# Scores of two tail heads in one run, bf16 maxima over partitions, a split last output, and a new order for five engines

## The chip, the cores and the metric

The kernel runs on one core of one Trainium2 chip. The metric is the device time of one execution in microseconds (us); every kernel is run several times and the median counts. Five engines work side by side, each through its own list of instructions in order: TensorE (PE; its weight loads are shown as PEld), VectorE (DVE), ScalarE (ACT), GpSimd (POOL) and SyncE (SP), which here only issues DMA transfers. A trace of one execution gives the start and the duration of each instruction.

## The reference, cut to what matters

```python
scores = scale * np.matmul(q, k.transpose(0, 1, 3, 2))     # B=4, H=8, S=576, D=64
a = softmax(np.where(causal, -1e9, scores))
local = np.matmul(a, v)
q_p = phi(q)                                                # elu(q) + 1
mem_out = (q_p @ M_prev) / (q_p . z_prev + 1e-6)
x = g * mem_out + (1 - g) * local                           # g = sigmoid(beta), per head
x = x.transpose(0, 2, 1, 3).reshape(2304, 512)
xn = x / sqrt(mean(x * x) + 1e-6) * rms_g
out = (silu(xn @ w_gate) * (xn @ w_val)) @ w_out            # 512 x 1536, 512 x 1536, 1536 x 512
```

## The kernel before, in words

The 2304 rows are cut into 18 blocks of 128. Each of the four sequences has 576 rows: four full blocks and 64 rows that are left. Two sequences share a **tail block**, so there are two of these, and in a tail block the upper 64 rows need the keys of one sequence and the lower 64 those of another. All matmuls of such a block therefore write 64 of the 128 output partitions, in pairs (`HALVES`); the text calls them half-column matmuls, since they use half of the array's columns.

A float32 product is made of three float16 products: each operand is split into a high and a low half (hi, lo), and hi·hi, hi·lo and lo·hi are added up in PSUM. Only the first four blocks run their attention in float32 (lines with `32` in their function's name). Before a split, a tensor is scaled by a power of two that a bound on its norms gives. For the bound, `gram` multiplies each tensor with itself on PE in bf16 (tile `csum`), DVE takes each partition's maximum (`mx`, `wmx`), and `over_partitions` spreads the maxima over all partitions: a matmul with the stationary operand `src[:, j]` repeated and an identity as the moving one (tile `allp`, L272).

A block and a group of heads are a unit of attention: `u_scores` (PE L626 for full blocks, L649 and L660 in `tail_scores`), a DVE instruction that scales, masks and reduces, `u_exp` on ACT (L689), `u_lo` (DVE L708, then one DMA transpose of the probabilities, tile `PT`), and `u_pv` (L739 to L741, and L757 for tail blocks). Memory reads are L794 (float32) and L855. Two blocks form a chunk of the MLP, nine chunks in all: `m_proj` (tile `gv`: 24 matmuls of 256 columns, float32 L1074 or float16 L1081), `m_act` (ACT L1098, DVE L1099 and L1102, which read the `gv` tile), `m_split` (hi and lo of the hidden layer, ACT L1119 and POOL L1120), `m_down` (tile `out`, L1147 or L1155 to L1157) and `put`, which scales the output into `res` and sends it.

PSUM has eight banks: the tags `sc`, `gv` and `out` have two each, and a tag's next tile waits until its bank's last reader is done. In a tail block each head takes one `sc` bank for the scores against the four full blocks of keys (16 matmuls) and then the other `sc` bank for those against the block's own rows (tile `sct`, 4 matmuls).

The order of each engine is written out by hand. `keep(kind)` puts a letter on the instructions that a function issues (S scores, P the product with V, M memory, G projection, D down projection and output DMA, Z `over_partitions`, l, m, b, d, W, B loads). The table `ISSUE` holds a string of such letters for each engine, and `issue_in_order` chains the instructions in that order: `S20` takes the next twenty of kind S, and `~n` skips n that are waiting.

Of the kernel before, what the change touches and what calls it, by code (L numbers as in the profile page):

```python
# [70 lines left out]
        "G3DGG2~1GD~1GDG4DGD3G5G2~3G4SG12S~7G5D~1GDG3D~1GD~2DG9S~7GS~7M~8SG3G~10MS~6GS2~6G5G~4GM2~7GG~2M~7S5S~1SM~7SDMM~6"
        "MM~5MGM2GMG2MG5S7G2SG4S2D~1GSGSG2S3MG3SGDG4DG12SG4SG3G2~1G9S6G8PZG5P2SGP4GPSP4S3P3SPSP2GP3GPGPG3SG14G2~3PGG~2S2G"
        "G3~1S2G~1G10S3S~1PM2S~1MGS~1S4MP3G2MPSGSPGP2MG~3MPGG~2GG2~1P2G~1PG5P4GP4GP2GPG4PGMGDG5DD2~1D2SDGD2~2MD~2D2MDG11D"
        "~2MGP2MPSGS~4SS~3P3G2MDPGSGDP3GS~2PS2MGSDGG~4DPG~4GMP5DPSPD~2G~3PG2P3GDMS~1GDGS3~1DS2DSG6PGDG3S2G3D~2GSG2SP8SGP3"
        "DPD2P10DS~1PS~1G~2D~3S~1G3~2PG~2GG~1GS~1DS~1SD2G3DGDGMD~3DG2D~2M2D~2GS~1GSGDG2M2G~6GSMDMSGDMG~4SG2SG~2G2SG2DG2D~"
        "1GMD~1SG3M2D~1MGD~4GDG3MDMGP5DP5GP7G2PGMD~1MPSP5SGDP3S~3DSGS~2GS~2DSDS2~1D~1P7DPSPSD2D~3DSG18D~2G3D~2G3S~5DG2SS~"
        "4GS2G2S2~2G3DPG3PGP2SPDP2GS~1PG3SPG5D2~2DPD~1DP5G~3PG~3S3G~3G3PG4S~4S3G4SG6DG3D~2PD~2G2DG~2GG4~1M2G2~1MG~1MD~1G~"
        "1P5MDGSPGMG2M2GPG2P2D~3P4GPS~4G3SP3SPG2SD~3SG2D2G~1GSG3MG2D~1DGSGSPDGP2S~2P2MP3GPG2PG~12GS2GPD~2PG4S2P2GSG2D~2SG"
        "~3G2PG6DMGMD~1MGM2P3SG2PSGDG2D~3G6P4MGPSPDPS3GSG2D3G2PSGDG3SGSGSGSG3SG4P3GDPDP2GPD~1PDGDG2P~1G~3P2G~3SG2SPSG~1PS"
        "~5G~1SGS~4P2SPS2PGSG5D~1G4PG5SG3D~1S2DGG2~1S4G2~1SG~1GD~1PGDGSPG2PDPD~1P2SPD~1P2SDGP4D~1GPSMS2GMP2GMD~1G4PG3D~1G"  # L80
# [33 lines left out]
    "Activation": (
        "K~2K~2K2fI~1T~1TITfT~1TE6ITE~2E~1E2E~1E~1EE~1E2U~3U~2U~19NU~1TU~12U~11NftTtU~15UTfET~1E~2E2U~8E~2E~1ETEUU~3TU~3E"
        "E~1E3UU~1UU~1U2E~1E2U~4U~1UoAU~12U2U~1oNU~1U~6U~4AUU~3U~2U2AU~4U~2U~1U2U~4U~4AUU~2U~1UXU~1UfUAUNU2AU2U~1UXc2U~1U"
        "cU2U~2AU~2cU~1UqAc2U~1UcU~1UxUcxUqxcxAcxU~1Ux2rxkxAU~1xkUxAcxkxFxcxAfxrxqAxHv3xAkE~1ECExFEACxO2HD~1HvAxvE2CAE2Dx"
        "CH~1E2AxHrCEyEkAyE~1CyH~1EfACNEyEHCv~1XFyqAEHyCEvCHAyEvrEyCHyNCAvfXysksyEHACqEFCAyEHrEC2HEO~1AEOCDHCAEHDANCXkEsH"
        "fECsAqCAFrHECE2CAHCEAHEC2HAECHNfAXksECsHAqFEHCEACrHEACECOHECAEOCHAENCsfHADXEskCHEACEAHCFEDCEHACsHseAqE~1EC2HvEAC"
        "HANXErAfCEHkAHCECkAHsAoECO~1FHEODCHAsE~1ECEAEvHvHCvDEAEs2HCAqE~1ECrHkfAHNAXFHs2AqfHArNECXECHE~1AkECHECEAFEHCsACs"  # L120
        "Es2CeEAHO~1qCOCAv~2DoHv~1Ev~1CE~1vAEvHDCHNCqAXECfErAHCEHACkAHkECHAFrHAkE~2HE~1ECEfNCEAqXE~2FE~1EHCACEHrAECHCAOE~"
        "1OD~2ECNHACfXkqHAE~1ECD~1HCAFErDHCEACHEAHCECAHECANfHXkAHAEFCECHAECEHACHO~1AECHOD~1E2CACHDAECHEACAHNECXECHAECHEAC"
        "HAHANXHAHAHAHOAHOAHAHDA2H2A2H2A2HADH2AHOD~2D~1D"
    ),
    "DVE": (
        ".~1f2.ZI~4JZIfI~3fS2.S2II~2I.~1IS2IS4TS2I2Su.2iSe~6SuSiTui2e~35u2iTiuie~26uiTi~1uiu~1iuiRU~1R2fJfZtZU~9S4UfS4Tfi"
# [1385 lines left out]
```

## Time and profile before

| | us |
|---|---|
| median of 3 runs | 594.09 (590.65, 594.09, 594.92) |
| the profiled execution | 592.08 |
| its span, first to last instruction | 590.4 |
| PE busy in the span | 577.9 |
| DVE, ACT, POOL busy | 427.4, 398.1, 129.3 |

The span is what the trace covers; the execution's own time is 1.7 us more. An engine is busy from an instruction's start to its end; matmuls overlap, so that PE's pitch (start to start) says more than the mean length of one. Views in use: busy time by stretch, waits by engine and line, the timeline, groups of instructions, and DMA issues.

### The profile page before, as it was taken

Reading aid. Unit: us, or ns where it says so; the run is one execution under the profiler, and the core shown is the slowest. Engines: PE = TensorE matmul, PEld = TensorE weight load, DVE = VectorE, ACT = ScalarE, POOL = GpSimd, SP = SyncE. Lnnn points to the kernel's source line nnn. Section 1 sums busy time; section 2 is a strip of 40 time slices with the busy share of each in tenths; the row PEclk is TensorE's granted clock in tenths of the full one; section 3 lists DMA queues with packets and bytes.
Section 4 is the critical chain, followed back from the end, with each engine's and each line's share of the span. In section 5 each row is a group of like instructions: output and inputs, shape, how many; then the busy total and the mean of one; then the engine's idle time right before and its main releaser. Section 6 shows DMA issues by size and latency. Waiting matters only on the chain.

```text
span 590.4 us, 15790 instructions
## 1 busy us (share of the span) xinstructions
PE 577.9 (98%) x6108; PEld 453.2 (77%) x6108; DVE 427.4 (72%) x1278; ACT 398.1 (67%) x856; POOL 129.3 (22%) x219
## 2 busy tenths in 40 slices
PE   8899999999999999999999999999999999999996
PEld 7898877678768778887777777777777777777773
DVE  5898779999998868776877676978866665742221
ACT  6899988878896757667667777866675555533211
POOL 2511100032332212121313231223122212121211
PEclk9999999999999999999999999999999999999999
DMA  8999794488598776887689678579685654340001
GB/s 264 326 374 382 251 225 114 83 189 206 116 166 162 145 138 133 151 157 144 104 156 180 140 127 166 118 134 156 117 172 84 91 110 100 69 87 19 18 1 54
DMA packets 183787, 87.57 MB, mean 148 GB/s; under 512 B 165792, under 2 KB 165792, under 8 KB 183712
## 3 DMA queue, kind: packets, MB, share of 16 engines
q1 hardware_dynamic: 180640, 81.82, 64.5%
q10 hardware_dynamic: 3072, 4.74, 2.5%
q8 instruction: 48, 0.79, 0.6%
q14 instruction: 27, 0.22, 0.1%
HBM read 37.77 MB, written 4.72 MB: 72 GB/s over the span
## 4 chain that ended last, share of the span: by engine, by line
PE 84%; DMA 9%; DVE 3%; ACT 2%; issue 1%; SPq 0%; ACTq 0%; DVEq 0%
PE gv L1081 38%; PE gv L1074 7%; PE out L1157 6%; PE out L1155 6%; PE out L1156 6%; PE sc L626 5%; DMA PT<-P 4%; PE out L1147 4%; DMA kv<-in_qkv_dram 2%; PE csum L299 2%; PE sc L649 1%; DMA M<-in_M_prev_dram 1%; PE loc L757 1%; PE loc L739 1%; PE loc L740 1%; PE loc L741 1%
## 5 line engine op out<-in xcount | busy, mean ns | idle before, releaser
L1081 PE MATMUL gv<-xT,wgv 128*128 128x256 f16 x2304 | 355.5, 273 | 0.6 <-DMA xT<-x 0.6
L1081 PEld LDWEIGHTS <-wgv 128*128 128x128 f16 x2304 | 209.5, 98 | 53.4 <-issue 3.5
L1120 POOL TENSOR_TENSOR h<-th,h 128x256 f16<-128x256 f32 x88 | 64.4, 734 | 258.4 <-ACT h L1119 224.7
L1098 ACT ACTIVATE th<-gv,wt 128x256 f32<-128x256 f32 x96 | 45.0, 469 | 71.6 <-PE gv L1081 68.2
L626 PE MATMUL sc<-kT,qT 128*128 128x128 f16 x576 | 91.7, 219 | 0.6 <-DMA qT<-qT 0.6
L1099 DVE SCALAR_TENSOR_TENSOR th<-th,gv 128x256 f32<-128x256 f32 x96 | 40.0, 417 | 71.0 <-ACT th L1098 69.3
L689 ACT ACTIVATE S<-S,nm 128x256 f32<-128x256 f32 (+3 forms) x112 | 70.3, 638 | 17.6 <-DVE nm L632 11.2
L708 DVE SCALAR_TENSOR_TENSOR P<-S,P 128x512 f16<-128x512 f32 (+2 forms) x96 | 65.6, 685 | 21.4 <-ACT P L203 21.3
L632 DVE CUSTOM_DVE_ANT_0 S<-sc,mask,qsc 128x256 f32<-128x256 f32 (+2 forms) x96 | 58.0, 613 | 15.3 <-PE sc L626 14.3
L1157 PE MATMUL out<-wo,h 128*128 128x512 f16 x176 | 65.8, 379 | 0.0
L1155 PE MATMUL out<-wo,h 128*128 128x512 f16 x176 | 65.6, 379 | 0.0
L203 ACT ACTIVATE P<-S 128x512 f16<-128x512 f32 (+2 forms) x96 | 58.1, 607 | 10.9 <-DMA PT<-P 7.4
L1156 PE MATMUL out<-wo,h 128*128 128x512 f16 x176 | 65.1, 379 | 0.0
L1119 ACT CAST h<-th 128x256 f16<-128x256 f32 x88 | 35.1, 399 | 42.3 <-DVE th L1102 28.0
L626 PEld LDWEIGHTS <-qT 128*128 128x128 f16 x576 | 51.9, 98 | 11.9 <-DMA qT<-qT 1.1
L739 PE MATMUL loc<-v,PT 128*128 128x65 f16 x288 | 50.6, 193 | 1.5 <-DMA PT<-P 1.4
L741 PE MATMUL loc<-v,PT 128*128 128x65 f16 x288 | 51.4, 193 | 0.0
L740 PE MATMUL loc<-v,PT 128*128 128x64 f16 x288 | 50.3, 193 | 0.0
L1074 PE MATMUL gv<-xT,wgv 128*128 128x256 f32 x192 | 47.3, 385 | 0.0
L1102 DVE SCALAR_TENSOR_TENSOR th<-th,wt,gv 128x256 f32<-128x256 f32 x96 | 45.7, 476 | 1.6
L1074 PEld LDWEIGHTS gv<-xT,wgv 128*128 128x128 f32 x192 | 34.7, 190 | 8.9 <-issue 4.5
L739 PEld LDWEIGHTS <-PT 128*128 128x128 f16 x288 | 28.0, 98 | 8.2 <-DMA PT<-P 2.8
(230 smaller groups left out, 988.4 us busy)
## 6 DMA issues: line engine op xcount, KB each, us to landing
kv<-in_qkv_dram SPq DMA_DIRECT2D x40, 256.0 KB, 3.9
q<-in_qkv_dram SPq DMA_DIRECT2D x18, 256.0 KB, 3.4
wo<-in_moe_w_out_dram SPq DMA_DIRECT2D x8, 512.0 KB, 5.1
out_dram<-res ACTq DMA_DIRECT2D x16, 256.0 KB, 2.9
wo<-in_moe_w_gate_dram SPq DMA_DIRECT2D x7, 512.0 KB, 6.8
wgv<-in_moe_w_val_dram SPq DMA_DIRECT2D x7, 512.0 KB, 7.3
qT<-qT SPq DMA_DIRECT2D x28, 128.0 KB, 2.8
wgv<-in_moe_w_gate_dram SPq DMA_DIRECT2D x5, 512.0 KB, 6.9
```

Of the source, the lines that this page charges most:

```text
L203: got = fn(*p, **k)
L626: nc.tensor.matmul(t[:, g * w + j * P : g * w + (j + 1) * P], qT[n][:, t2, h, :], kT[blk_of[(b, j)]][:, h, :], start=(t2 == 0), stop=(t2 = ...
L632: nc.vector.tensor_tensor_reduce(out=s[:, g * w : (g + 1) * w], in0=t[:, g * w : (g + 1) * w], in1=mask[:, m0 : m0 + w], scale=qsc[n][:, 5 ...
L689: nc.scalar.activation(v_, v_, AF.Exp, bias=nm[:, g : g + 1], scale=-1.0)
L708: m = nc.vector.scalar_tensor_tensor(out=p16[:, w : 2 * w], in0=s[:, :w], scalar=PSCALE, in1=p16[:, :w], op0=ALU.mult, op1=ALU.subtract)
L739: nc.tensor.matmul(a, phi_, vhi, start=(j == 0), stop=False)
L1074: nc.tensor.matmul(o, wgv[:, 1 + p, o0 : o0 + P], xT[0][:, cc, at], start=(cc == 0), stop=(cc == NC - 1))
L1081: nc.tensor.matmul(o, lhs, xT[c][:, rhs, :], start=(cnt == 0), stop=(cnt == 3 * NC - 1))
L1120: nc.gpsimd.tensor_tensor(h16[:, 1], th, h16[:, 0], ALU.subtract)
L1155: nc.tensor.matmul(o, hh, whi, start=(f == 0), stop=False)
L1156: nc.tensor.matmul(o, hh, wlo, start=False, stop=False)
L1157: nc.tensor.matmul(o, hl, whi, start=False, stop=(f == NF - 1))
```

## The change

There are four edits. The first one is a new `ISSUE` string for each of the five engines.

The second takes the identity as bf16 wherever `over_partitions` gets a bf16 source, and `stat_end` (for the first two sequences) and `gv_scales` write their maxima as bf16. Ten of the fifteen `allp` matmuls of 128 columns change so; five stay float32.

The third makes an even head of a tail block compute the scores of that head and the next one, 32 half-column matmuls into two `sc` banks, and the own-row scores of both, 8 matmuls, into one bank of the tag `gv`. The odd head's call takes its two banks from `sc2`.

The fourth splits the last chunk's second output block in two halves of 256 columns in two banks, one of the `out` tag and a new tile `end` in an `sc` bank. Half 0 leaves PSUM by ACT and is sent by SP, half 1 by DVE and is sent by ACT. The block's 36 matmuls of 512 columns become 72 of 256.

```diff
@@ ISSUE
     "PE": (
-        "w5T3T4~1w4ZTsT4s2ZsT8SS~1S~2SS~2S3uT3T~1SS~1S~2S~3T2~1T2uS4T2u2hTT~1Th3Tsu2~2T2h3Thu2T3h4TsTsTsTs~4h4s~4T2s~4R2s"
+        "w8T3sT5sT4ZwTZTT~2sT5S3S~1S~2S3T2uT2SS~1S~2S~3T4uS4T2u2ThTs~1hs~1ThThTu~2u~2T2h4uTuT2s~1h4TT~3Ts~1T3h4s~5TRTRs~5"
...
@@ over_partitions
         t = ps.tile([P, 512], F32, tag="sc", name="allp")
+        one = ident if src.dtype == F32 else ident.bitcast(BF16)[:, 1::2]
         for j in range(n):
             nc.tensor.matmul(
-                t[:, j * P : j * P + P], src[:, j : j + 1].to_broadcast([P, P]), ident, start=True, stop=True
+                t[:, j * P : j * P + P], src[:, j : j + 1].to_broadcast([P, P]), one, start=True, stop=True
             )
@@ stat_end
-        nc.vector.tensor_reduce(mx, stt[b], axis=AX.X, op=ALU.max)
+        if b < 2:
+            near = mx.bitcast(BF16)[:, :2]
+            nc.vector.tensor_reduce(near, stt[b][:, :2], axis=AX.X, op=ALU.max)
+        else:
+            nc.vector.tensor_reduce(mx, stt[b], axis=AX.X, op=ALU.max)
...
@@ u_scores
-        if n < NA and h0:
+        if n < NA and h0 or i == NI and h0 % 2:
             t = sc2.pop(n)
@@ tail_scores
-        for j in range(NI):
-            for t2 in range(2):
-                for bb, r in enumerate(HALVES):
-                    nc.tensor.matmul(
-                        t[r, j * P : (j + 1) * P], qT[n][:, t2, h, r],
-                        kT[blk_of[(b + bb, j)]][:, h, :], start=(t2 == 0), stop=(t2 == 1),
-                    )
+        if h % 2:
+            t, own = t
+        else:
+            own = ps.tile([P, 512], F32, tag="gv", name="sct")
+            two = (t, ps.tile([P, 512], F32, tag="sc", name="sc"))
+            for x, o in enumerate(two):
+                for j in range(NI):
+                    for t2 in range(2):
+                        for bb, r in enumerate(HALVES):
+                            nc.tensor.matmul(
+                                o[r, j * P : (j + 1) * P], qT[n][:, t2, h + x, r],
+                                kT[blk_of[(b + bb, j)]][:, h + x, :], start=(t2 == 0), stop=(t2 == 1),
+                            )
+            for x in range(2):
+                for t2 in range(2):
+                    for r in HALVES:
+                        nc.tensor.matmul(
+                            own[r, x * P : x * P + P], qT[n][:, t2, h + x, r], kT[n][:, h + x, :],
+                            start=(t2 == 0), stop=(t2 == 1),
+                        )
+            sc2[n] = two[1], own
...
-        t = ps.tile([P, 512], F32, tag="sc", name="sct")
...
@@ gv_scales
-        mx = tiny.tile([P, 2], F32, tag="mx", name="wmx", bufs=2)
+        mx = tiny.tile([P, 2], F32, tag="mx", name="wmx", bufs=2).bitcast(BF16)[:, :2]
@@ put
-        end = c == NCHUNK - 1 and tb == 1
-        if end:
-            nc.vector.tensor_scalar(res, outp[c, tb], scale, None, op0=ALU.mult)
-        else:
-            nc.scalar.activation(res, outp[c, tb], AF.Copy, scale=scale)
+        if half == 1:
+            nc.vector.tensor_scalar(res, outp[c, tb][1][:, at], scale, None, op0=ALU.mult)
+        else:
+            o = outp[c, tb] if half is None else outp[c, tb][0]
+            nc.scalar.activation(res, o[:, at], AF.Copy, scale=scale)
+        queue = nc.sync if half == 0 else nc.scalar
...
@@ m_down
+            if c == NCHUNK - 1:
+                outp[c, 1] = outp[c, 1], ps.tile([P, DM], F32, tag="sc", name="end")
...
```

What the new strings do is seen in three places. The first is SP's list at the start of the program (`kv` are rows of k or v, `q` of q, `in_M_prev` the memory, `in_moe_w_gate` the weights). Before:

```order
L363 DMA kv_106<-in_qkv_dram 128x512
L405 DMA q_104<-in_qkv_dram 128x512
L405 DMA q_109<-in_qkv_dram 128x512
L374 DMA wo<-in_M_prev_dram 64x512
L363 DMA kv_111<-in_qkv_dram 128x512
L389 DMA kv_2_0_204<-in_qkv_dram 128x512
L374 DMA wo<-in_M_prev_dram 64x512 x2
```

Of the change:

```order
L377 DMA kv_106<-in_qkv_dram 128x512
L419 DMA q_104<-in_qkv_dram 128x512
L377 DMA kv_111<-in_qkv_dram 128x512
L419 DMA q_109<-in_qkv_dram 128x512
L388 DMA wo<-in_M_prev_dram 64x512 x3
```

The second block's keys (`kv_111`) come ahead of its queries, and three pieces of the memory behind them in a row. Further down, the first piece of the weights comes behind two more loads of q, k or v, and the second behind four more.

The second place is DVE's list in the first tail block (`sc`, `sct` are score banks, `gv` a projection's, `th` the hidden layer). Before:

```order
L653 ISA S,nm<-sc,mask,qsc 128x512
L653 ISA nm 128x1
L663 ISA S,nm<-sct,tmask,nm,qsc 128x128
L663 ISA nm 128x1
L1099 SCALAR_TENSOR_TENSOR th<-th,gv_4099 128x256
L1102 SCALAR_TENSOR_TENSOR th<-th,wt,gv_4099 128x256
```

Of the change:

```order
L1126 SCALAR_TENSOR_TENSOR th<-th,gv_4292 128x256
L273 TENSOR_SCALAR pw<-ss 128x2
L1129 SCALAR_TENSOR_TENSOR th<-th,wt,gv_4292 128x256
L690 ISA S,nm<-sct,tmask,nm,qsc 128x128
L690 ISA nm 128x1
```

The own-row reduction (L663, now L690) no longer stands right behind the main one. It comes behind the two activation steps of a projection, and the bank that it reads is one of the projections' two.

The third place is the end of ACT's list. Before:

```order
L1132 ACTIVATE res<-out_0_9469,wos 128x512
L203 DMA out_dram<-res 64x512 x2
L203 DMA out_dram<-res 128x512
```

Of the change:

```order
L1160 ACTIVATE res<-out_1_9462,wos 128x256
L216 DMA out_dram<-res 64x256
L1160 ACTIVATE res<-out_0_9461,wos 128x512
L216 DMA out_dram<-res 64x256
L216 DMA out_dram<-res 128x512
```

One of the small transfers now stands ahead of the last eviction, which is that of the full block; half 0's two transfers went to SP, and half 1's two are ACT's.

## Rows read from the trace of the kernel before

**Rows 1.** The page: busy us (share) and instructions of PE; granted clock in tenths
```profile
PE 577.9 (98%) x6108; PEld 453.2 (77%) x6108; DVE 427.4 (72%) x1278; ACT 398.1 (67%) x856; POOL 129.3 (22%) x219
PEclk9999999999999999999999999999999999999999
```
**Rows 2.** Stretches: from:to, length, busy of PE PEld DVE ACT POOL, clock, DMA, GB/s
```profile
0.00:45.00 45.00, 41.06 (x320) 36.56 (x320) 34.24 (x158) 37.35 (x114) 13.89 (x33) 1.00 0.98 322
270.00:320.00 50.00, 49.67 (x760) 38.23 (x755) 37.43 (x109) 34.17 (x68) 10.65 (x15) 1.00 0.78 132
480.00:530.00 50.00, 50.00 (x774) 38.38 (x773) 30.38 (x85) 23.61 (x44) 9.66 (x16) 1.00 0.45 91
585.00:590.40 5.40, 0.00 (x0) 0.00 (x0) 0.56 (x1) 0.69 (x1) 0.00 (x0) 0.78 0.35 97
```
**Rows 3.** Waits of PE: us in total, times, longest us
```profile
PE busy L291 <- POOL ident L307: 1.5, 1, 1.5
PE loc L739 <- DMA PT<-P: 1.4, 4, 0.6
PE xtp L916 <- DVE diag L911: 1.3, 2, 0.9
```
**Rows 4.** Waits of PE's weight loads, the same columns
```profile
PEld L739 <- DMA PT<-P: 2.8, 5, 0.7
```
**Rows 5.** Timeline of PE, weights' gram and allp: start us, us, line
```profile
73.06 0.44 PE L272 MATMUL allp<-ident,mx 128*128 128x128 f32 x2
73.33 0.85 PE L299 MATMUL csum<-wgv 128*128 128x128 bf16 x12
74.02 0.44 PE L272 MATMUL allp<-ident,wmx 128*128 128x128 f32 x2
```
**Rows 6.** Timeline of PE, two more allp matmuls
```profile
61.23 0.38 PE L272 MATMUL allp<-ident,mx 128*128 128x128 f32 x2
61.45 0.28 PE L299 MATMUL csum<-kv 128*128 128x128 bf16 x2
```
**Rows 7.** Timeline of PE, a run of 20 half-column matmuls
```profile
280.42 0.49 PE L1081 MATMUL gv<-xT,wgv 128*128 128x256 f16 x3
280.84 0.64 PE L649 MATMUL sc<-kT,qT 128*64 128x128 f16 x16
...
281.52 0.28 PE L1081 MATMUL gv<-xT,wgv 128*128 128x256 f16 x1
```
**Rows 8.** Timeline of PE, full matmuls of 256 columns
```profile
284.96 1.36 PE L1081 MATMUL gv<-xT,wgv 128*128 128x256 f16 x11
286.16 0.38 PE L1155 MATMUL out<-wo,h 128*128 128x512 f16 x1
```
**Rows 9.** Timeline of PE, a run of 120 half-column matmuls of 65 columns
```profile
525.12 2.10 PE L757 MATMUL loc<-v,PT 128*64 128x65 f16 x120
527.14 0.39 PE L1157 MATMUL out<-wo,h 128*128 128x512 f16 x1
```
**Rows 10.** Groups of ACT and DVE: shapes, count, busy us, mean ns, idle before
```profile
L1098 ACT ACTIVATE th<-gv,wt 128x256 f32<-128x256 f32 x96 | 45.0, 469 | 71.6 <-PE gv L1081 68.2 <-PE loc L741 1.9 <-POOL h L1120 0.8
L1099 DVE SCALAR_TENSOR_TENSOR th<-th,gv 128x256 f32<-128x256 f32 x96 | 40.0, 417 | 71.0 <-ACT th L1098 69.3 <-POOL h L1120 1.2
L1102 DVE SCALAR_TENSOR_TENSOR th<-th,wt,gv 128x256 f32<-128x256 f32 x96 | 45.7, 476 | 1.6
```
**Rows 11.** Timeline of the end, all engines
```profile
584.39 0.59 PE L1157 MATMUL out<-wo,h 128*128 128x512 f16 x2
584.81 0.75 DVE L1130 TENSOR_SCALAR res<-out,wos 128x512 f32<-128x512 f32 x1 [1.84 <-PE out L1157]
585.03 0.69 ACT L1132 ACTIVATE res<-out,wos 128x512 f32<-128x512 f32 x1 [1.56 <-PE out L1157]
585.60 1.77 ACTq L203 DMA_DIRECT2D out_dram<-res  x3
```
**Rows 12.** DMA issues: count, KB each, median us to landing
```profile
out_dram<-res ACTq DMA_DIRECT2D x16, 256.0 KB, 2.9
```

More of the change, by code (lines that the diff above doesn't have):

```diff
@@ L71 @@
[L71 to L80, printed above, removed]
@@ new lines @@
+        "3s~4s~4s~4s~4s4G2g8g~8g3Gg2Gg3GG~3G~3g4Ggg~10gg~9g~9gg~8g~8Zgg~7g5g~2g2G~2Z~1g7g~2g~2gZg~1Zg4G~2gg~9g~9g~9g~9gg~"
+        "8g~8g~8g~8g~8g4g~4Gg2Ggg~1g~1gG2g2Zg2GZgGg12Dg3D~1ZDG3D~1D~2G~5DG2G~3G~3G2ZG3D~2D2G2D~1G~1D~2G3DG4DGD2G7DG~1G~1G"
+        "~1G~1G~1G~1G~1G~1G~1D~1G3SG4S~7G2DG6DS~7G2S~7GS~7D~1SG6SG5SG2SGS2S~1S3MG4M~7SM~7M~7M~7M~7M~7M2G~4GG~3G~3GMGMGMG2"
+        "SMSMSG4SDM2SG2S2GSG4D~1S2G2S2G5S4G2DG3DG19G~1G~1G4S2G2S3G3S2G3SG5PGP3G2P7GZG2P2S5P2SGP2GP4G4SG2SPG4PG4SG5SGG~2G~"
+        "2G~2G3SG2PG9S2G2S~3S2P2S~1PGPGMSPMS3MSM2SGG~4GSG~3G~3P4GMG~2G~2P2G~2GG~1G~1G~1G~1DGMPD~2MP7GP3GP2G5DG6D~1D~1DGD~"
@@ new lines @@
+        "3D2D~1D~1DM3GD~3DG11MGSG2P4DMPGS~5P3S~5S3GS~2MDGG~6MP2G~6S~2G2PS3D2PSG2MDD~2G~2P3G~2P5S2GG~1D~2P2S2DSDGDGPG11DD~"
+        "2S~1S~1SG2SGP~1P~1SP~1P~1P~1P~1P~1SG2P~1SP~1P~1P~1GDP~1D~1DP~1P~1P~1P~1P~1P~1P~1P~1P~1P~1DSP~1SP~1G~1PSG~1DG~1G~"
+        "1D~2D~2G~1G~1G5SDGD~1SDD~3D~3DG3DMGMG2M2GS~1MDSD~1SMGMG~5MSDGSG~4G~4G2SG~2G~2SGDG~1G2D~1G5D~1D~1M3GMG2SGMPDS~5P4"
+        "D~3MG2PSP2MP4GDGP3DP2D~1PDGDP2GPDPMPSP4GDS~3S~3GPS~3S~3SD~1DP6SPSPDSDD~3DG16SG2DD~1G3SS~4GS~4G~2G4S~4D~1SG2SGS~2"
+        "G2SDSGD~3GP2GP2GDP2SPGPG2SG5D~2DP2G~4D~1DP3GPSG~3P2SG~3GPG~2G~2G~2G~2SG~2G~2G~2G~2DG4SGPG5SGD~2GD~2DG~3G~3G~3G~3"
@@ new lines @@
+        "MSG~3G~3G~3G~3M2P4SMG~3GD~1GPMG~1G~1PMG~1G~1PG~1PD~4G~1S~5P2GPGP2G2PGMPMSP2SDSPGSG2D2S~1D~1G~2G5SGD2G2SGSD~3GPMP"
+        "2S~2P3D~3P2GMGPS~2PG3DP3G6S~2PG~4D~2SS~1GS~1G~3G2S~1MG~1G~1G2SP2G3MGM2P2G3MGDG7D~4P2DMP2DSPGPSPDPSD~1S2G2SG2D2G3"
+        "PG2PG4SGSD~3SGSG4SPSPDGP2DPSD~1GP2G2G~4GP~1P~1D~1G~3G2DSGP~1SGS~5SS~4P~1P~1P~1SP~1SP~1SP~1SG4PG4D~3DG8SDG3S3G~2G"
+        "~2GG~1S~2SG~1D~1PG~1S~1PG~1PGDPSGSGPSDD~3D~3GP3GPSP2MPSPSMGPMPDSGPG9PG2PMG2PDP4MGPGM2PMPGDG5PGDG3SG3D2G~8G2SMS~6"
+        "DGDSGSDSPG2SPGSGS~1DGMGP4GSPGPGPSP2G4PSG2SGDS2G2S~1GD2GPGS~1GP2GS~1G~4G~4S~1GSGS2GG~1SPSP3G~1G~1G~1P3DPDG~1PG~1G"
@@ new lines @@
+        "PGSPGPGMGDPGPSGPM2G2P2M2D~3PGMG2P2GSGG~3G2S3DS~2G~1G~1G~1S~2SGSPDG3PSPDPG3DP2S~5P4GDSD~3GPGDS~4DPG10P~1G~1SDP~1P"
+        "~1P~1G~1P~1G2P~1PDP5GPS~3GS~3G2SG3DPS~2S2GS2G2SGG~10G6P2DG2P3SPS~7D~2GDPSP2SDSPS~4SPG~1G~1SDG~1S2PG~1G~1S2G3SMSG"
+        "DS~2P3SP3G3PSPG2P2G2PG8P2MP2GPDD~2P4GP2G2DMGPSDGMG3M2GMGSG2S~5DD~1MGSGD~1DG2SMG2D~1GG~4G~4G~4SD~1G~4PGS~2GG~2SPG"
+        "SP4GPG2DPGP2SP2SDPGSG2S2G3PG2D~3G2MG~6GSPGMSGP2GPSP2GDGPGD~2PDSPGPS2G2PGMGPSPDG3MS~2GDSP3D~3PGPMG2S~1P2MS~1P2GS~"
+        "1MGSG3DG2SG~3D~2PGSP2G~2GPGPGSPGPS~1GD~2PS~1PGSDS2G2SP2G2PG2PS2G3D~4SDG6PDP3D~2DGP2G~2D~1G~2GP4GS32PGD~4PGP4DP3G"
@@ new lines @@
+        "7DG3PG2P2DG4PG3PG~1G~1D~1PG~1P2GP3G2PGPG3PG4DD~1G2YP2G3P2GP5G~5PGP2GPG~3GG~2G~2G2DD~2DG2S~8S~8S~8S~8S~20S~20S~8S"
+        "~8S~8S~8S~8S~8S~8S~8S~8S~8S~8S~8S~8S~8S~8S~8S~8S~8S~8S~8S~8S~8S~8S~8S~8S~8M4S6M2S2M10D~1G3PG4G~11D~1GDG4G~6G6D~3"
+        "G2DG4DGD~1GS8DG4DG2G~8S19G3DG2DG~3GG~2GG~1G5D2G3DGDG5DG3D~2PS2P2SP2S2PS2P3SPSPSP3SPSPSP44S~8S~8S~8S~8S~8S~8S~8S~"
+        "8S~8S~8S~8S~8S~8S~8S~8S~9S~9S~9S~9S~9PS~9S~9P2S~9P2S~9PS~8PS~8P2S~8S~8P4S~8P2S~8P2S~8P2S~8P11G2DGDG~1G4DG2D2G5DG"
+        "12DGD2G5M16P30S8GD~1D~1G3DG16D~1GD~1G6D~1S~8G4S~8S8G5S2GDG3S2S~2G~3G~3SG~3G~3G~3SG~3GG~2DS2G~2GSG~1GDG3D2GSDSDSD"
@@ L113 @@
+        "~2D~2DD~2D~1D3D~3D~3D~3D~3D~3D~3D3"
     ),
     "Activation": (
[L115 to L123, printed above, removed]
+        "K~1K~2K~1fKTI~1T2fT~1TEE~1EIEE~2E2E~1E~1ETEE~1EE~1EIEU~2U~2NU~13TU~18TNft2U~12U2TfE3TETU~9U~13E4TU~4U~3U~3E5U~1U"
@@ L148 @@
+        "2kbFkrll~1lr~1rkL2bFL2l~2rLr2kLl2Ll~1LFlblLXLlrL2Xr~1rkL2l~1lFL2rbLrL3krLXL2Fl~1blL2rLrLXLkrL2FlLrlL2rLrLXLbLl~1"
+        "klm~1LmL2FL3XrLr2k2blL2lL2FLbl2L3rkl2r~1rXFbrLXLr2kLlLlm~1mLFL4bL4XrL2kr~1rkLFbr3kL2XFL4brL2Xr2LkL2FL2rL2Xr~1LrL"
+        "kL3FL8X2D~1D"
     ),
@@ L458, in stat_end @@
         mx = tiny.tile([P, 3], F32, tag="mx", name=f"mx{b}", bufs=2)
-        nc.vector.tensor_reduce(mx, stt[b], axis=AX.X, op=ALU.max)
+        if b < 2:
[3 more added lines that the diff above has]
+            nc.vector.tensor_reduce(mx, stt[b], axis=AX.X, op=ALU.max)
         c = cb[b]
         if b < 2:
-            nc.vector.tensor_scalar(mx[:, :2], over_partitions(mx[:, :2], 2), 1.03, None, op0=ALU.mult)
+            nc.vector.tensor_scalar(mx[:, :2], over_partitions(near, 2), 1.03, None, op0=ALU.mult)
             pow2_scales(mx[:, :2], 2, c[:, 0:2], c[:, 3:5])
@@ L656, in tail_scores @@
         )
-        t = ps.tile([P, 512], F32, tag="sc", name="sct")
-        for t2 in range(2):
-            for r in HALVES:
-                nc.tensor.matmul(
-                    t[r, :P], qT[n][:, t2, h, r], kT[n][:, h, :], start=(t2 == 0), stop=(t2 == 1)
-                )
+        at = h % 2 * P
         nc.vector.tensor_tensor_reduce(
-            out=s[:, w : w + P], in0=t[:, :P], in1=tmask, scale=qsc[n][:, 5:6],
+            out=s[:, w : w + P], in0=own[:, at : at + P], in1=tmask, scale=qsc[n][:, 5:6],
             scalar=nm[:, 0:1], op0=ALU.add, op1=ALU.min, accum_out=nm[:, 1:2],
@@ L1123, in put @@
     @keep("O")
-    def put(c, tb, scale):
+    def put(c, tb, scale, half=None):
         if tb == 0:
             outp["res"] = sb.tile([P, 2 * DM], F32, tag="res", name="res", bufs=1)
-        res = outp["res"][:, tb * DM : (tb + 1) * DM]
-        end = c == NCHUNK - 1 and tb == 1
-        if end:
-            nc.vector.tensor_scalar(res, outp[c, tb], scale, None, op0=ALU.mult)
-        else:
-            nc.scalar.activation(res, outp[c, tb], AF.Copy, scale=scale)
+        at = slice(0, DM) if half is None else slice(half * DM // 2, (half + 1) * DM // 2)
+        res = outp["res"][:, tb * DM : (tb + 1) * DM][:, at]
+        if half == 1:
+            nc.vector.tensor_scalar(res, outp[c, tb][1][:, at], scale, None, op0=ALU.mult)
+        else:
+            o = outp[c, tb] if half is None else outp[c, tb][0]
+            nc.scalar.activation(res, o[:, at], AF.Copy, scale=scale)
+        queue = nc.sync if half == 0 else nc.scalar
         for p0, np_, b, s0 in rows_of(2 * c + tb):
-            keep("D")(nc.scalar.dma_start)(out=out[b * S + s0 : b * S + s0 + np_, :], in_=res[p0 : p0 + np_])
+            keep("D")(queue.dma_start)(out=out[b * S + s0 : b * S + s0 + np_, at], in_=res[p0 : p0 + np_])
     @keep("D")
@@ L1154, in m_down @@
             hl = h16[:, 1, tb * P : tb * P + P]
-            nc.tensor.matmul(o, hh, whi, start=(f == 0), stop=False)
-            nc.tensor.matmul(o, hh, wlo, start=False, stop=False)
-            nc.tensor.matmul(o, hl, whi, start=False, stop=(f == NF - 1))
-            if f == NF - 1:
-                put(c, tb, wos[:, 7:8])
+            for half in (0, 1) if type(o) is tuple else (None,):
+                at = slice(0, DM) if half is None else slice(half * DM // 2, (half + 1) * DM // 2)
+                for lhs, rhs in ((hh, whi), (hh, wlo), (hl, whi)):
+                    nc.tensor.matmul(
+                        (o if half is None else o[half])[:, at], lhs, rhs[:, at],
+                        start=(f == 0 and rhs is whi and lhs is hh), stop=(f == NF - 1 and lhs is hl),
+                    )
+                if f == NF - 1:
+                    put(c, tb, wos[:, 7:8], half)
     @keep("K")
```

108 lines of the change are left out of this document (55 added, 53 removed).

## The prediction

> **What bounds the kernel now.** I read the page first: PE is busy 577.9 of 590.4 us and the clock is granted in full throughout [rows 1]. Then the stretches, to see whether one of them has another limit. The two stretches in which the tail blocks' scores run, 270 to 320 and 480 to 530 us, have PE at 49.67 and 50.00 of 50; DVE is at 37 and 30 there [rows 2]. So a DVE instruction that is moved costs nothing by itself, and PE work that is taken away is taken from the time, unless a wait comes in its place. PE is idle in two places: 45 − 41.06 = 3.9 us in the first 45 us, and the 5.4 us behind the last matmul [rows 2]. In all it idles 590.4 − 577.9 = 12.5, so some 12.5 − 3.9 − 5.4 = 3.2 us are left for the 540 us between. The waits name them: 1.5 us at the start for the identity that POOL makes, 1.3 for DVE's diagonals, 1.4 for transposed probabilities [rows 3], while the weight loads ahead of the same matmuls waited 2.8 for the latter [rows 4]. The kernel is one long list of matmuls; everything below is counted in what that list loses or gains. The profiled execution took 592.08, 2.0 less than the median of 594.09; I make the sum against 592.08 and add the 2.0.
>
> **Maxima in bf16.** A float32 matmul shows as two records: `allp` x2 at 73.06 is one matmul, from 73.06 to 73.33, 0.27 us, and the next at 74.02 follows twelve bf16 matmuls of as many columns that took 0.69 together, 0.058 each [rows 5]. Ten such matmuls go from the one price to the other: 10 × (0.27 − 0.058) = **−2.1**. Where two float32 ones stood close, one took 61.45 − 61.23 = 0.22 [rows 6], so −1.6 is the other end. The first lies at 61 us, behind the start's waits, and the 3.2 us of idle time behind it can't absorb much, so the gain stays.
>
> **Two heads in one run.** Going from full matmuls to pairs of half-column ones and back costs PE something. In [rows 7] three projections of 0.109 each (1.20 over eleven [rows 8]) start at 280.42, so the run of 20 (16 and the 4 own scores) should start at 280.75; it starts at 280.84, 0.09 late. From there to the next full matmul are 0.68; ten pairs of 128 columns at 0.058 are 0.58, so 0.10 goes at the end. That is 0.19 a run. Along the two PE orders I count 18 such runs before and 14 after, of all kinds (scores, own scores, PV, memory): 4 × 0.19 = **−0.8**, not the eight runs that eight joined heads suggest, since the own scores now stand apart in several places. Against that, the new order mixes scores with PV matmuls within a run. A pair of PV halves takes 2.02 / 60 = 0.034 [rows 9], 0.024 less than a pair of scores; where one half of a pair is a score, the other gains nothing. In some 25 places the order pairs a PV with a score: up to 25 × 0.024 = 0.6, nothing if the halves overlap freely; I take **+0.3**, the middle. The 36 matmuls of 512 columns that become 72 of 256 move as many columns; at 0.109 for 256 that is no cost.
>
> **The bank of the own scores.** `sct` now takes one of the two `gv` banks, eight times. A projection's bank is free when ACT and DVE have read it, 0.469 + 0.417 + 0.476 = 1.36 us [rows 10]. While `sct` holds one, projections have the other, and a projection of 24 matmuls lasts 24 × 0.109 = 2.6, longer than 1.36; what comes between two projections on PE (down projections, PV) covers it also. But DVE reaches the own-row reduction late in the new order, behind other work. Between nothing and 1.36 at each of eight places (10.9), I take the end near nothing, **+0.4**, because DVE is idle a quarter of these stretches [rows 2].
>
> **The order in the middle.** What can go wrong is that PE arrives at a unit's PV before its transposed probabilities. I summed PE's pitches along both orders from a unit's last score to its first PV: less than 10 us lie between in 10 of the 96 full units before, in 18 after (mean 14.3 and 13.1 us). Before, ten such units cost 1.4 us on PE, 2.8 by the weight loads [rows 3, 4]; at 0.28 a unit, eighteen would cost 5.0, 2.2 more. At the other end the DVE, ACT and SP orders were moved along with PE's and nothing is added. I take **+1.4**, nearer to the row.
>
> **The start.** SP's order brings the second block's keys ahead of its queries, three pieces of the memory in a row, and the first weight piece behind two more loads of attention rows. PE's work ahead of the first projection is nearly the same (0.5 us more). The identity's 1.5 stays. At best the rest of the idle goes, −(3.9 − 1.5) = −2.4; at worst the weights are late by the two 256 KB loads more that I count ahead of them, 512 KB at 322 GB/s = 1.6 [rows 2]. I take **−0.5**, near the middle.
>
> **The end.** The last matmul ends at 584.39 + 0.59 = 584.98 = T. DVE ends its eviction at 585.56 and ACT's three issues start at 585.60, 0.59 each, so the third, the full block's, starts at 586.78, T + 1.8 [rows 11]; the span ends 3.6 later. After the change, half 1 is out of PSUM before T, since the full block's three matmuls come last: ACT issues its first transfer then, evicts the full block (0.69), issues the second transfer meanwhile, and can start the third when the eviction is done, at T + 0.4 + 0.7 = T + 1.1. **−0.7**. The full block's 256 KB (2.9 us [rows 12]) stay the last to land. The ends are 0, if ACT's issues don't overlap its eviction, and −1.0, if ACT is through with its first issue at T. A page of the Trainium skill speaks against more: "DMA: Bandwidth & Descriptors", section "Issuing engines are not separate DMA queues", says that transfers started by several engines run on the same 16 DMA engines and interleave, so a second issuer saves only the time of issuing. By that rule the two queues save two issues of 0.59 at most and no transfer time; no row here shows two queues at once.
>
> **Sum.** −2.1 − 0.8 + 0.3 + 0.4 + 1.4 − 0.5 − 0.7 = −2.0. The profiled execution would take 590.1, the median **592.1**. With the terms' ends, few of them at once, this case reaches from 588.5 to 596.
>
> **Rivals.** *The order was moved so that waits vanish.* The four known gains, −2.1 − 0.8 + 0.3 − 0.7 = −3.3, come with both rests of idle time, 2.4 at the start and 3.2 between: −8.9, a median of 585.2. For it: PE's waits are few and named [rows 3], each is an operand a little late, and an order can cure that. Against it: the distances to PV shrink. *The same with late operands.* With PV's waits at +2.2 and the start at +1.6 the sum is −2.1 − 0.8 + 0.3 + 0.4 + 2.2 + 1.6 − 0.7 = +0.9: 595.0. For it are the eight closer units, against it that each of its terms stands at its end. Here too belongs that joining heads doesn't do what it says, if runs cost the same whatever their number: the sum is then −1.2. *On the other side: the projections wait for a bank.* If DVE, which reads the own scores behind two activation steps of a projection, holds each of the eight `gv` banks until PE stands at the next projection, PE loses one activation chain each time: −2.0 − 0.4 + 8 × 1.36 = +8.5, a median of 602.6. It decides from about 1.04 us a place, where −2.4 + 8 × 1.04 reaches 5.9. For it: with one bank left, a projection can't start before the last one's readers are done, and PE has no slack there [rows 2]. Against it: the projections are spread among other matmuls in PE's order.
>
> **How the numbers follow.** Forecast 0.55, waits vanish 0.20, late operands 0.13, bank held 0.12. What a measurement of this kernel can tell from no change is about 1%, 5.9 us: below 588.2 or above 600.0. Faster gets 0.16 of the second case and 0.05 from the forecast's lower edge, 0.21; slower gets 0.12 and 0.01 from late operands, 0.13; 0.66 is left within. The range of 8 in 10 takes the forecast's and the late case's spread and reaches to most of the fast one: 586.0 to 598.5; the held bank and the fast case's lower part stay outside.
>
> **What would show it.** In the profile after: `allp` of `mx` and `wmx` near 0.06 with one record each; 14 half-column runs with 0.19 around each; the third ACT issue about 1.1 us behind the last matmul; PE's waits for `PT` up from 1.4, and none of more than 0.5 us of a `gv` matmul for DVE. The prediction is wrong if `gv` waits for DVE in the tail stretches sum to over 5 us, if `PT` waits pass 4, or if the first 45 us change by over 3.

## The result, and the profile after

The change is faster: 587.74 us in the median of 6 runs (586.66 to 588.18) against 594.02 for the kernel before in the same session, a ratio of 0.990 (0.987 to 0.993), 6.3 us. Measured again in a second session it took 587.63 against 592.48, ratio 0.991 (0.988 to 0.994), 4.9 us. The forecast had the sign, the range held the time, and the size was under half of what was measured. The profiled execution took 588.12, with a span of 586.2.

The page and four stretches, the columns as in [rows 1, 2]:

```profile
PE 575.6 (98%) x6134; PEld 455.4 (78%) x6134; DVE 426.3 (73%) x1278; ACT 399.7 (68%) x857; POOL 132.4 (23%) x219
```

```profile
0.00:45.00 45.00, 42.12 (x329) 38.27 (x330) 33.99 (x158) 37.88 (x116) 14.05 (x33) 1.00 0.95 322
270.00:320.00 50.00, 49.83 (x745) 38.19 (x744) 37.31 (x109) 32.67 (x66) 10.07 (x15) 1.00 0.70 122
480.00:530.00 50.00, 50.00 (x776) 38.98 (x775) 29.60 (x84) 25.13 (x46) 11.79 (x18) 1.00 0.49 88
581.90:586.20 4.30, 0.00 (x0) 0.00 (x0) 0.00 (x0) 0.69 (x1) 0.00 (x0) 1.00 0.43 122
```

PE is still the bound, and the clock granted in these stretches is 1.00. Its busy time fell by 577.9 − 575.6 = 2.3 us, and the span by 4.2. The waits of PE, to set beside [rows 3]:

```profile
PE loc L766 <- DMA PT<-P: 2.0, 5, 1.0
PE busy L305 <- POOL ident L321: 1.5, 1, 1.5
PE allp L286 <- ACT junk L424: 0.9, 1, 0.9
PE mem L882 <- DVE t L910: 0.7, 1, 0.7
PE sc L644 <- DMA qT<-qT: 0.6, 1, 0.6
PE xtp L943 <- DVE few L1210: 0.3, 1, 0.3
```

This is the whole list that the view gives. No projection (`gv`) stands in it, neither for a bank nor for DVE; the rival of the held bank needed eight such waits. The maxima on PE's timeline, beside [rows 5]:

```profile
72.09 0.22 PE L286 MATMUL allp<-ident,mx 128*128 128x128 bf16 x1
72.14 0.74 PE L313 MATMUL csum<-wgv 128*128 128x128 bf16 x10
```

One record now, and the next matmul starts 0.05 later instead of 0.27. The joined heads, beside [rows 7]:

```profile
267.45 0.27 PE L1108 MATMUL gv<-xT,wgv 128*128 128x256 f16 x1
267.65 1.08 PE L673 MATMUL sc<-kT,qT 128*64 128x128 f16 x32
268.67 0.20 PE L768 MATMUL loc<-v,PT 128*128 128x65 f16 x1
```

Sixteen pairs take 1.02 us to the next full matmul, 0.12 more than 16 × 0.056, and the entry costs the same 0.09 as before: so a run of 32 costs around it what a run of 20 did. The end, beside [rows 11]:

```profile
581.08 0.81 PE L1189 MATMUL out<-wo,h 128*128 128x512 f16 x3
581.28 0.48 DVE L1157 TENSOR_SCALAR res<-end,wos 128x256 f32<-128x256 f32 x1 [2.08 <-PE end L1189]
581.46 1.15 SPq L216 DMA_DIRECT2D out_dram<-res  x2
581.80 0.49 ACTq L216 DMA_DIRECT2D out_dram<-res  x1
582.34 0.69 ACT L1160 ACTIVATE res<-out,wos 128x512 f32<-128x512 f32 x1 [0.91 <-PE out L1189]
582.36 1.21 ACTq L216 DMA_DIRECT2D out_dram<-res  x2
```

The last matmul ends at 581.89 and ACT's third issue starts at 583.06, 1.2 later, where it was 1.8 before and the prediction had put it at 1.1. The span ends 4.3 us behind the last matmul instead of 5.4.

### The profile page after: what moved, and what is told of

Same layout as the page of the kernel before. It is cut to its first block, busy times and chain, and to the rows that moved or that the text cites. A ratio compares the mean times of both kernels' runs of the same rounds, so it can differ in the third digit from the quotient of the medians.

```text
span 586.2 us, 15844 instructions
## 1 busy us (share of the span) xinstructions
PE 575.6 (98%) x6134; PEld 455.4 (78%) x6134; DVE 426.3 (73%) x1278; ACT 399.7 (68%) x857; POOL 132.4 (23%) x219
## 4 chain that ended last, share of the span: by engine, by line
PE 84%; DMA 8%; DVE 5%; issue 1%; ACT 1%; SPq 0%; POOL 0%; ACTq 0%; POOLq 0%; DVEq 0%
PE gv L1108 37%; PE out L1189 19%; PE gv L1101 7%; PE sc L644 5%; DMA PT<-P 4%; PE out L1178 3%; DMA wgv<-in_moe_w_val_dram 2%; PE csum L313 2%; PE loc L784 1%; PE sc L673 1%; PE loc L766 1%; PE loc L768 1%; PE loc L767 1%; PE mem L882 1%; DMA qT<-qT 1%; PE tp L567 1%
## 5 line engine op out<-in xcount | busy, mean ns | idle before, releaser
L1189 PE MATMUL out<-wo,h 128*128 128x512 f16 (+1 forms) x528 | 173.7, 372 | 0.0
L1147 POOL TENSOR_TENSOR h<-th,h 128x256 f16<-128x256 f32 x88 | 66.8, 761 | 251.2 <-ACT h L1146 219.8
L644 PE MATMUL sc<-kT,qT 128*128 128x128 f16 x576 | 95.9, 219 | 0.6 <-DMA qT<-qT 0.6
L735 DVE SCALAR_TENSOR_TENSOR P<-S,P 128x512 f16<-128x512 f32 (+2 forms) x96 | 67.5, 703 | 25.1 <-ACT P L216 24.4
L1189 PEld LDWEIGHTS <-h 128*128 128x128 f16 x564 | 54.2, 98 | 13.2
L766 PE MATMUL loc<-v,PT 128*128 128x65 f16 x288 | 51.9, 193 | 2.0 <-DMA PT<-P 2.0
L767 PE MATMUL loc<-v,PT 128*128 128x64 f16 x288 | 52.0, 193 | 0.0
L768 PE MATMUL loc<-v,PT 128*128 128x65 f16 x288 | 51.7, 193 | 0.0
L913 POOL TENSOR_TENSOR t<-t,t 128x256 f32<-128x256 f32 x28 | 21.6, 775 | 65.4 <-DVE t L910 42.9
```

The source lines that it names most:

```text
L644: nc.tensor.matmul(t[:, g * w + j * P : g * w + (j + 1) * P], qT[n][:, t2, h, :], kT[blk_of[(b, j)]][:, h, :], start=(t2 == 0), stop=(t2 = ...
L735: m = nc.vector.scalar_tensor_tensor(out=p16[:, w : 2 * w], in0=s[:, :w], scalar=PSCALE, in1=p16[:, :w], op0=ALU.mult, op1=ALU.subtract)
L766: nc.tensor.matmul(a, phi_, vhi, start=(j == 0), stop=False)
L767: nc.tensor.matmul(a[:, :D], phi_, vlo, start=False, stop=False)
L768: nc.tensor.matmul(a, plo, vhi, start=False, stop=(j == nb - 1))
L1147: nc.gpsimd.tensor_tensor(h16[:, 1], th, h16[:, 0], ALU.subtract)
```

## The experiments

**Two of the edits in the old order.** The ends of ACT's and SP's strings are the only part of the order that follows.

```diff
+        one = ident if src.dtype == F32 else ident.bitcast(BF16)[:, 1::2]   # and bf16 mx, wmx
-  (ACT) ...ADH2AHOD~2D~1D
+  (ACT) ...ADH2AHO~1D~2OD~1D          # put and m_down with halves, as in the change
```

> The kernel before with two of the four edits: bf16 maxima, and the last output in two banks and queues (the ends of ACT's and SP's lists follow the change's); order and tail scores as before. Theory (the edits carry their own terms into any order): ten allp matmuls shrink by 1.6 us in sum, as the two traces show, and the stretch behind the last matmul by 1.1 (5.4 to 4.3); 2.7 us faster than before, ratio 0.9955. Rival (the new order is what makes them count): PE or the output waits for something else at once, at most 0.5 us faster.

590.29 against 592.59, ratio 0.997 (0.9953 to 0.9987): 1.8 us by the ratio and 2.3 by the medians, inside the theory's reach and far from the change's.

**The new order and joined heads without these two edits.**

```diff
-        one = ident if src.dtype == F32 else ident.bitcast(BF16)[:, 1::2]   # float32 mx, wmx again
-            for half in (0, 1) if type(o) is tuple else (None,):             # one 512-column output again
```

> The change without those two edits: float32 maxima and a whole last output by DVE and ACT's queue, all in the new order and with joined tail heads. Theory: it loses the same 2.7 us against the change and keeps what order and joined heads give, 6.3 - 2.7 = 3.6 us faster than before, ratio 0.994. Rival: the order alone gives no more than the traces show in idle time of PE and half-column runs, 0.8 + 0.8 = 1.6 faster, ratio 0.997.

591.66, ratio 0.9995 (0.9976 to 1.0014): 0.3 us by the ratio and 0.9 by the medians. Both sides fall. The two halves of the change give 1.8 and 0.3 (2.3 and 0.9), and together 5 to 6: more than their sum. That was the question from here on.

**The kernel before, twice more.** No edit.

> The kernel before, unchanged, for a second profile, since its executions lie between 590.7 and 595.2 us and those of the change between 586.7 and 588.2. Theory: the executions differ by waits of PE for transfers, in the first 45 us or for transposed probabilities; PE's busy time stays at 577.9 within 0.3 and its idle time takes the whole difference. Rival: the matmuls themselves are slower over the whole span, and PE's busy time grows.

> The kernel before once more, for a third profile: theory and rival as in the run ahead of it. If the waits are at a fixed place, it is the same place in both.

They took 591.70 and 595.00. In the first, the first 45 us have PE at 42.13, as the change has it; the 1.1 us that PE waits more in [rows 2] are not in every execution. The second waits at one place, 270.6 us, and this is how it goes on (from:to, length, PE PEld DVE ACT POOL, clock, DMA, GB/s):

```profile
270.00:272.00 2.00, 1.01 (x14) 0.40 (x8) 1.63 (x6) 0.29 (x1) 0.67 (x1) 1.00 1.07 175
272.00:274.00 2.00, 1.05 (x8) 0.79 (x9) 0.72 (x2) 1.02 (x2) 0.00 (x0) 0.73 0.84 185
274.00:276.00 2.00, 2.00 (x29) 1.61 (x27) 0.77 (x2) 0.22 (x2) 0.00 (x0) 0.50 0.19 38
276.00:278.00 2.00, 2.00 (x20) 1.44 (x19) 0.83 (x5) 0.97 (x3) 0.42 (x1) 0.92 1.10 198
```

```profile
272.94 0.24 PE L739 MATMUL loc<-v,PT 128*128 128x65 f16 x1 [1.93 <-DMA PT<-P]
```

PE waits 1.93 us for transposed probabilities, and behind it the granted clock is at the lower level, 1.2 GHz, from about 272.9 to 276.3. By the two traces set beside each other, matmul by matmul, the place costs 3.0 us: some 1.5 of wait beyond the other execution's, and as much again in slower matmuls (PE busy 580.2 instead of 578.5). The theory holds for one half of it, and the rival for the other, though its slower matmuls stand at this place alone and not over the whole span.

**The change again, with two of its edits undone alone.**

> The change, unchanged, beside the kernel before on one chip with its variants: the two partial kernels gave 1.8 and 0.3 us, the change itself 6.3 in an earlier session. Theory (the terms add up): some 2 to 4 us faster than before, ratio 0.994 to 0.996, and the earlier 6.3 had a part of two sessions' scatter in it. Rival (the edits and the order need each other): 6 us again, ratio 0.990.

587.63, ratio 0.991 (0.988 to 0.994): the rival. Only float32 maxima back in the change:

```diff
-        one = ident if src.dtype == F32 else ident.bitcast(BF16)[:, 1::2]   # float32 mx, wmx again
```

> The change with float32 maxima (ten allp matmuls of two passes again), nothing else undone. Theory: 1.6 us slower than the change, the sum of the ten in the two traces. Rival: later waits move, and it is more than 3 us slower or not slower at all.

592.65 (591.82 to 594.08), ratio to the kernel before 1.0003 (0.9984 to 1.0022): 5.0 slower than the change, the rival again, for 1.9 us of matmul time (the `allp` of `mx` and `wmx` take 2.69 us of PE instead of 0.81). The lists of both kernels are the same but for these matmuls, so the two traces can be laid side by side: matmul by matmul, the lag is 1.5 us at 93 us, behind the ten, 1.6 at 270, 2.9 at 342, 2.0 at 400, 3.2 at 490 and 4.9 from 524 on. It falls between 342 and 400, where the change has small waits of its own. Beside the change's other profile (588.12) the lag ends at 3.7, so that some 1 us of it is one execution's scatter. The four longest of PE's waits show what came in; in two profiles of the change the first row has 2.0 and 1.0, the third 0.6 and none, and the fourth isn't there:

```profile
PE loc L761 <- DMA PT<-P: 2.9, 6, 1.0
PE busy L304 <- POOL ident L320: 1.5, 1, 1.5
PE sc L639 <- DMA qT<-qT: 1.2, 1, 1.2
PE out L1184 <- ACT h L1141: 1.0, 1, 1.0
```

Only the last output whole again:

```diff
-            for half in (0, 1) if type(o) is tuple else (None,):
+            # one bank, 36 matmuls of 512 columns; DVE evicts, ACT's queue sends 2 x 64 rows
```

> The change with the last output block whole again: 36 matmuls of 512 columns, one eviction on DVE, two transfers by ACT's queue ahead of the full block's eviction, none by SP. Theory (the order of ACT's list is what shortens the end, since the full block's issue starts at 1.1 instead of 1.8 us behind the last matmul): within 0.7 us of the change. Rival (two banks and a second queue do it): 1.1 us slower, with 5.4 us behind the last matmul.

588.39 (0.9922, 0.989 to 0.9953), 0.8 more than the change, between theory and rival and within the scatter of both; the stretch behind the last matmul is 4.9 us in the profile. So, by one profile of this kernel, 0.5 of the 1.1 us at the end is ACT's new order and 0.6 the split.

```profile
580.28 0.75 DVE L1158 TENSOR_SCALAR res<-out,wos 128x512 f32<-128x512 f32 x1 [1.95 <-PE out L1185]
580.51 0.38 PE L1185 MATMUL out<-wo,h 128*128 128x512 f16 x1
581.06 0.48 ACTq L216 DMA_DIRECT2D out_dram<-res  x1
581.67 0.69 ACT L1160 ACTIVATE res<-out,wos 128x512 f32<-128x512 f32 x1 [2.85 <-DVE res L1158]
581.69 1.15 ACTq L216 DMA_DIRECT2D out_dram<-res  x2
```

The trace shows half of why the split counts: DVE's eviction of 512 columns ends at 581.03, ACT issues its first transfer only then, and the full block's eviction behind it starts 0.78 us after the last matmul's end (580.89), where in the run of the change it is 0.44; the third issue follows, 1.5 after the last matmul instead of 1.2. The other 0.3 lies between that issue and the end: the block lands 2.35 us after its issue, 2.2 in both profiles of the change, and the program ends 1.1 after the landing instead of 1.0.

**The loads ahead of the late transpose.**

```diff
-  (SP) ...rk l~1l L2 m LFL3...
+  (SP) ...rk L l~1l L m LFL3...
```

> The kernel before with one place of SP's list changed: the two loads of 256 KB issued at 264.6 us come behind the transpose of probabilities that was issued at 266.9, not ahead of it. In two of four profiles of the old order PE waits some 2 us for that transpose at 270.5 and its granted clock is at half for 3 us behind it. Theory (the loads make the transpose late, and the wait lowers the clock): the wait goes, the clock stays at 1.00 there, 1.5 us faster than before, and no execution over 592.5. Rival (other transfers or the transpose itself are the cause): same time, same scatter.

592.94, ratio 0.9998 (0.9975 to 1.0022), up to 596.9: the rival's time. Its one profile has only 0.3 us of wait at 270; so have two of the four profiles of the old order, and whether the late wait is gone from all executions isn't shown. PE waits elsewhere, with the clock at 1.00:

```profile
PE gv L1081 <- DVE th L1102: 1.9, 1, 1.9
```

This is 7 us further on, and none of the other five profiles of the old order has it. The trace tells where it comes from: a load of the memory (`M`), issued behind the moved loads, lands after 6.2 us, where it took 3.0 to 3.3 in four profiles of the old order; ACT waits 2.4 us for it, and the activation steps (`th`) that PE's next projection needs come behind that. So the moved loads met another transfer. That they made the transpose late is not shown by it.

**More matmuls, without float32.**

```diff
             nc.tensor.matmul(t[:, j * P : j * P + P], src..., one, ...)
+            if one is not ident:
+                for again in range(3):
+                    nc.tensor.matmul(t[:, j * P : j * P + P], src..., one, ...)   # same result, same place
```

> The change with each of the ten bf16 allp matmuls issued four times into the same place (30 more of 0.058 us, 1.7 us of PE work at the places where float32 cost 1.6 more). Theory (what a later PE does to the rest, not float32, makes the 5 us of the float32 variant: it meets its transposes and transfers in another phase): 4 to 5 us slower than the change, with PE waits between 485 and 530 us as there. Rival (float32 itself does it): 1.7 slower and no wait there.

593.69 (591.17 to 597.15), ratio to the kernel before 1.0021 (1.0004 to 1.0038): about 6 us slower than the change (587.63 in the session before), for 1.7 of work. So float32 itself isn't needed for the loss; later matmuls are enough. The profiled execution, the longest of them at 597.15, has

```profile
PE loc L775 <- DMA PT<-P: 3.2, 4, 1.0
PE out L1198 <- ACT h L1155: 2.5, 1, 2.5
```

and the lower clock behind the wait of 2.5 (0.51 of full speed from 528 to 530 us). What ACT waits for there, in the stretch from 514 to 530 us, stands the same way in three kernels (us, times, longest): the change, its float32 variant, this one:

```profile
ACT P L216 <- DMA PT<-P: 1.4, 2, 1.2
```

```profile
ACT P L216 <- DMA PT<-P: 2.7, 1, 2.7
```

```profile
ACT P L216 <- DMA PT<-P: 4.2, 1, 4.2
```

ACT can't write a unit's probabilities before the transpose of an earlier unit has read that buffer; that transpose is in flight with two outputs of 256 KB. In the change it is issued 0.70 us behind the second of them, in the other two 0.02 and 0.03. The outputs' landing times, each the middle of two, in the same order:

```profile
out_dram<-res ACTq DMA_DIRECT2D x2, 256.0 KB, 3.7
```

```profile
out_dram<-res ACTq DMA_DIRECT2D x2, 256.0 KB, 5.2
```

```profile
out_dram<-res ACTq DMA_DIRECT2D x2, 256.0 KB, 5.9
```

Only the second output is late: the first lands 3.2, 3.6 and 3.5 us after its issue, the second 4.2, 6.8 and 8.3, and the transpose issued beside it 5.0, 7.0 and 8.5. The kernel of the second experiment, with float32 maxima and a whole last output, shows the same: 0.03 us apart, 6.2 and 6.5 us, and ACT waits 2.3. In the change's other profile they are 1.2 us apart, and take 3.7 and 4.1. That the distance in time decides it was not tried by itself.

**These outputs later.** In the float32 variant, and in the change:

```diff
-  (ACT) ...NECECAHD~1XDECECHAHANXHA...
+  (ACT) ...NECECAHXECECHAHAD~1DNXHA...
```

> The float32 variant of the change with the two output transfers of the last chunk but one (256 KB each, issued at 515.3 and 515.7 us there) moved in ACT's list behind two units' exponentials and four activation steps, to about 527. In the float32 variant ACT waits 2.7 us at 520 for a transpose that was in flight with them, and PE 1.0 for ACT behind it. Theory (transfers that share the DMA engines with the transposes make these late): ACT's wait falls to 1.3, PE's wait of 1.0 goes, 1.0 to 1.5 us faster than the float32 variant, 591.3. Rival (the transposes are late by themselves): same waits, 592.7.

> The change with the same two output transfers moved. The change has no PE wait between 480 and 530 us, so by the theory of the run ahead there is nothing to win: within 0.5 us of the change. Rival (a transfer that is moved meets the last transposes of x at 522 instead): 1 us slower.

The float32 variant falls from 592.65 to 590.00 between two sessions, its ratio to the kernel before from 1.0003 (0.9984 to 1.0022) to 0.9958 (0.9942 to 0.9974), 2.6 us; ACT's wait for the transpose is gone altogether, and from 485 to 530 us PE is left with

```profile
PE loc L761 <- DMA PT<-P: 0.3, 1, 0.3
```

where it had 1.7. The transfers at that place were the cause of that wait. The gain is larger than expected; 1.4 of it by the traces is at this place, the rest in waits for `qT` and `PT` before it that differ between executions. The change itself stays where it was, 588.10 (0.9927, 0.9901 to 0.9953): where PE has no wait, moving the transfer brings nothing.

**More matmuls in the old order.**

```diff
             nc.tensor.matmul(t[:, j * P : j * P + P], src..., ident, ...)
+            if n == 2:
+                nc.tensor.matmul(t[:, j * P : j * P + P], src..., ident, ...)     # same result, same place
```

> The kernel before, in its own order, with each of the ten float32 allp matmuls issued twice into the same place: 10 x 0.22 to 0.27 = 2.2 to 2.7 us more PE work at the places that the change shortens. Theory (only the new order is finely set to the shorter maxima, since the old order was set to float32 ones and gains only 1.8 from bf16 and the new end): also the old order is thrown off, 4 us slower or more, with new waits for transposes. Rival (the old order has more room): 2.5 slower and no more.

595.56, ratio 1.0057 (1.0037 to 1.0076): 3.3 us (2.2 to 4.5), for 2.2 us of added work (the `allp` of `mx` and `wmx` take 5.06 us of PE instead of 2.82). It falls between theory and rival and nearer to the rival: the old order passes on what is added and some 1.1 more, the new one about three times what is added.

## Why the prediction was right, and where not

- **What bounds the kernel**: right. PE's list is the time, and no term of the sum came from another engine.
- **Maxima in bf16**: −2.1 as work, and 2.82 − 0.81 = 2.0 us of PE time it is, from the traces before and after. As the price of the edit it was too small: taken out of the new order alone, it costs 5.0 us, since the waits behind it grow when PE arrives 1.8 us later. The step said that the gain stays; it didn't ask what else the shift moves.
- **Two heads in one run**: 18 and 14 runs, as counted; together with the mixing, all such runs take 21.45 us before and 20.68 after by the two traces, with what is lost around them: 0.77 less, where −0.8 + 0.3 was taken. Four runs fewer at 0.21 would be 0.84, so that the mixed runs cost less than 0.1 in sum. No run undid this edit alone.
- **The bank of the own scores**: +0.4 was taken, nothing is seen. DVE does read the own scores late, but no `gv` matmul waits; the rival at 602.6 falls.
- **The order in the middle**: this step failed. It counted units with under 10 us between scores and PV, 10 before and 18 after, and put 0.28 us on each. PE's waits for `PT` are 1.4 before [rows 3] and 2.0 and 1.0 in two profiles of the change, and its idle time from 45 to 480 us is 3.2, 3.2 and 4.5 in three profiles of the kernel before, 3.4 and 2.4 in two of the change. By the means the term is −0.7, not +1.4; the −0.7 is no more than what executions of one kernel differ by. In the other profiles before, PE's waits for `PT` are 1.6 and 3.1, so that they don't grow with the eighteen closer units. The distance in PE's list doesn't say whether a transpose is late; what is in flight with it can, as the moved outputs show at one place.
- **The start**: −0.5 was taken; 3.9, 2.9 and 3.2 us of idle time in three profiles before, 2.9 and 2.9 after: −0.5 by the means, and nothing beside the best execution before. The 1.3 us for DVE's diagonals, which the prediction named among the waits of the 540 us between, lie in these first 45; they fell to 0.3, and 0.9 at an `allp` that waits for ACT came in.
- **The end**: −0.7 was taken for ACT's issues and came out right to the tenth (1.84 to 1.16 behind the last matmul); with what follows it is −1.1. A page of the Trainium skill, "DMA: Bandwidth & Descriptors", section "Issuing engines are not separate DMA queues", says that a second issuer saves issue time alone. The trace agrees for half of the split's 0.6 us, which is the full block's issue coming 0.3 earlier; the other 0.3, behind that issue, the rule doesn't give, and with one profile of the undone split it may be scatter of the landing.

With the measured terms the sum is −2.0 − 0.8 − 0.7 − 0.5 − 1.1 = −5.1. The two sessions gave 4.9 and 6.3. This sum says where the traces differ, not what each edit is worth alone: the runs that undo edits show that the terms don't add up. Of the 3.1 us between forecast and sum, 2.1 are the order in the middle, 0.4 each the bank and the end, and 0.3 the mixing, less 0.1 for the maxima. The low clock behind the wait at 270.6 us may be in what the medians have beyond it: two of the six profiles in the old order show it there, and of the eight in the new order none but that with more matmuls shows one, at 528. It was not tried by itself. The measured time lies between the forecast and the fast rival (585.2), but waits that vanish in a moved order are not what happened: of the 5.6 us of idle time that the rival took away, 1.2 went by the means, and the larger part of the gain is work that PE no longer has and the shorter end.

What stays open is why the second output and the transpose land 2 to 4 us later when they are issued at the same moment, whether the waits at 342 and 490 us have the same cause, and what the new order and the joined heads give apart, since no run has one without the other.

## What to carry to other kernels

In this kernel, whose order is fixed by hand, an edit's price was the work plus what its shift did to the transfers behind it: 1.7 us of added matmuls cost 6 in the new order, 2.2 us cost 3.3 in the old one. Lay two traces of the same lists side by side and look where the lag grows, then look at what the DMA engines carry there. Here a transpose that ACT waited for wanted no 256 KB output issued beside it.

## What the runs showed of the hardware

A PE wait of 1.9 us was followed by 3.4 us at the lower granted clock (1.2 GHz) in two kernels of the old order, and one of 2.5 us in the change with more matmuls; a wait of 1.9 us 7 us further on in another kernel, and one of 1.6 in the old order with more matmuls, were not. Where the two executions were set side by side, the lower clock doubled the wait's price. And a run of half-column matmuls costs about 0.21 us around it, 0.09 at its start and 0.12 at its end: so for runs of 8 (four pairs take 0.35 us to the next full matmul, and 4 × 0.056 are 0.22), of 20 and 32, and of 120, whose pairs follow each other at 0.032. A 256 KB output and a transpose issued within 0.03 us of each other landed after 6.2 to 8.5 us in three kernels, and after 3.7 to 5.0 where 0.7 or 1.2 us lay between them.
